# Two W1 quarters and all keys and values of a batch in single runs of TensorE, from the third batch on

## The chip, the cores and the metric

The kernel runs on one core of one Trainium2 chip. The metric is the device time of one execution in microseconds (us). A core has five engines that run side by side, each through its own queue in order: TensorE (PE; its weight loads are listed as PEld), VectorE (DVE), ScalarE (ACT), GpSimd (POOL) and SyncE (SP), which here issues the DMA transfers.

## The reference

Three layers are computed one after the other for 8 batches of 576 tokens, in float32.

```python
# attention over 32 memory slots per head (8 heads of 64)
a = exp(phi - max_s(phi));  a = a / (sum_s(a) + 1e-9)
k_m = einsum('bhsm,bhsd->bhmd', a, k)
v_m = einsum('bhsm,bhsd->bhmd', a, v)
attn = softmax(q @ k_m^T / sqrt(64))
x = (attn @ v_m) as [batch, 576, 512]
# first layer block
xn = (x - mean) / sqrt(var + 1e-6) * g_ln
x = x + relu(xn @ w_ch1) @ w_ch2          # 512 -> 2048 -> 512
# second block: h = gelu(x @ w_in); u, v = halves of h
out = x + (u * (w_sg @ norm(v) + b_sg)) @ w_out
```

## The kernel before, in words

The kernel has two phases. Phase 1 does attention and the first block; phase 2 the second block. The change touches phase 1 alone.

**The stream of matmuls.** Phase 1 folds the attention's output projection into the weights: for each batch, the batch's values v_m are multiplied with W1 (scaled by g_ln and centred), in four quarters of 512 columns, by `make_vw`. The result, the tiles `VW`, is the weight of the first layer: `m1(j, c)` computes 128 hidden columns of a block of 256 or 320 tokens (six matmuls into `ph`, line 557), `m2` the second layer (three matmuls per token tile into a bank `py`, lines 587 to 589), three steps (LAG) behind `m1`. A batch has two blocks of 16 steps. The steps of all batches follow each other in one long stream on PE. In a batch from 1 to 6 each block goes through all four quarters, in the order TURNS (0, 1, 2, 3 in even batches, 3, 2, 1, 0 in odd ones), so the last two quarters of one batch are the first two of the next, and their W1 tiles stay in SBUF. The other two are loaded anew by `load_wc` (two tiles of 512 KB for a quarter; the pool has four such tiles, two quarters).

**The preparation of a batch** is spread between these steps. Every piece of it has a time in units of a plan, 18 units to a batch: `at_time(time, function)`, and `run_until` calls what is due between two steps. For batch b: `load_phi` and `load_kv` (keys and values of the first 512 tokens, four tiles n = 0 to 3, two transfers each), `load_rem` (the last 64 of the 576 tokens, "kvr"), `prep_max` (transposes into pt), `prep_exp` (mb, then exp), `prep_sum` (sums of the exponentials on POOL, two transposes into ptsum, then reciprocals rs), `prep_kv` for each half g of the heads (k_m and v_m into kvp, divided by the sums in `prep_norm`), `prep_T` (ptk, giving kvT), the scores `t_scores`, `t_norm`, `t_attn`, `t_x` (px) of each group of query tiles, and `make_vw` for each quarter.

**Small parts of the array.** Most matmuls use the whole 128 x 128 array. Three kinds use parts: `t_scores` and `make_vw` eight parts of 64 rows and 32 columns, `prep_kv` four parts of 128 rows and 32 columns for the first 512 tokens (c = 0 to 3) and, for the last 64 tokens (c = 4), parts of 64 rows, rows 64 g to 64 g + 63 of the tiles phir and kvr. These operands are plain float32, and each matmul shows as two instructions in the trace. So a W1 quarter is 16 instructions, one half of keys and values 40 (32 and then 8). All instructions of such a run are made to wait for the same things (`add_manual_dep`), so that it stands together.

**Banks.** PSUM has eight banks: two for `ph` (ps_h), four for `py` (ps_y, tags y0 to y3; the tile t of 128 tokens uses bank t mod 4), and two, pool ps_a with the one tag "a", that all of the preparation shares in the order of the plan: pt, mb, ptsum, kvp and ptk take one of them, px one, the scores and a W1 quarter both. A tile gets its bank when the tile that had it before has been read for the last time. A W1 quarter is evicted by one ACT copy (line 514) and one DVE subtraction (line 515) for each of its two banks, and cleared ahead of its run by two small DVE memsets (line 499, "claims").

**Order.** The order of instructions on each engine is made from the order of the program by a scheduler that simulates the run; `tc.issue_after(x)` keeps an instruction behind x on its engine. So an engine's order is fixed in the program that runs, and an engine waits where a semaphore is late.

Of the kernel before, what the change touches and what calls it, by code (L numbers as in the profile page):

```python
# [28 lines left out]
def fused_kernel(ctx: ExitStack, tc: tile.TileContext, q, k, v, phi, g1, w1, w2, w_in, g2, w_sg, b_sg, w_out, out):  # L29
# [5 lines left out]
    DM = H * D  # L35
# [16 lines left out]
    LAG = 3  # L52
    BESIDE = 7
    SCALE = 1.0 / math.sqrt(D)

# [85 lines left out]
    def phase1():  # L141
# [32 lines left out]
        def load_phi(b, gs):  # L174
            if gs[0] == 0:
                st["phi", b] = (
                    at.tile([P, H, 4, NM], F32, tag="phi", name="phi"),
                    at.tile([P, 4, NM], F32, tag="phir", name="phir"),
                )
            ph, pr = st["phi", b]  # L180
            hs = slice(4 * gs[0], 4 * gs[-1] + 4)
            with behind_w2(b, 5):
                load(ph[:, hs], phi[b, hs, 0:4 * P, :].rearrange("h (p c) m -> p h c m", c=4))
                for g in gs:
                    load(pr[REM * g:REM * g + REM], phi[b, 4 * g:4 * g + 4, 4 * P:S, :].rearrange("h p m -> p h m"))

        def load_kv(b, g, part):
            n = 2 * g + part
            if b == 0 and n >= 2:
                t = tail.tile([P, 2, 4, 2, D], F32, tag="vw", name="kv", bufs=VTAIL)  # L190
            else:
                t = at2.tile([P, 2, 4, 2, D], F32, tag="kv", name="kv")
            hs = slice(4 * g, 4 * g + 4)
            ins = []
            with behind_w2(b, 7 + n):
                for i, src in enumerate((k, v)):
                    src = src[b, hs, 0:4 * P, :].rearrange("h (p c) d -> p h c d", c=4)
                    ins.append(load(t[:, i], src[:, :, 2 * part:2 * part + 2, :]).ins.name)
            st["kv", b, g, part] = t, ins
# [40 lines left out]
        def prep_max(b, gs):  # L240
# [4 lines left out]
            with tc.issue_after(st["hl"].ins) if b else ExitStack():  # L245
                V.tensor_reduce(out=pm, in_=ph[:, hs].rearrange("p h c m -> p h m c"), axis=AX.X, op=ALU.max)
                for i, g in enumerate(gs):
                    rows, sub = slice(REM * g, REM * g + REM), slice(4 * i, 4 * i + 4)
                    V.tensor_tensor(out=pm[rows, sub], in0=pm[rows, sub], in1=pr[rows], op=ALU.max)
            pt = ps_of(b, [P, n, P], "pt")  # L250
# [9 lines left out]
        def prep_exp(b, gs):  # L260
# [5 lines left out]
            for i, g in enumerate(gs):  # L266
                rows, sub = slice(REM * g, REM * g + REM), slice(4 * i, 4 * i + 4)
                V.tensor_tensor(out=pr[rows], in0=pr[rows], in1=mb[rows, sub], op=ALU.subtract)
            rows = slice(REM * gs[0], REM * gs[-1] + REM)
            A.activation(ph[:, hs], ph[:, hs], AF.Exp)  # L270
            A.activation(pr[rows], pr[rows], AF.Exp)

        def prep_sum(b):
# [5 lines left out]
            for g in range(2):  # L279
                rows, sub = slice(REM * g, REM * g + REM), slice(4 * g, 4 * g + 4)  # L280
                G.tensor_tensor(out=sm[rows, sub], in0=sm[rows, sub], in1=pr[rows], op=ALU.add)
            pt = ps_of(b, [P, 2, P], "ptsum")
# [7 lines left out]

        def prep_kv(b, g):
            ph, pr = st["phi", b]
            kvp = ps_a.tile([P, 2, D], F32, tag="a", name="kvp")
            ts = [st.pop(("kv", b, g, part)) for part in range(2)]
            lands = [n for t in (*ts, st["kvr", b]) for n in t[1]] if b else []
            rows = slice(REM * g, REM * g + REM)
            for c in range(5):
                for j in range(4):
                    mm = PE.matmul(  # L299
                        kvp[32 * j:32 * j + 32],  # L300
                        ph[:, 4 * g + j, c, :] if c < 4 else pr[rows, j, :],
                        ts[c // 2][0][:, :, j, c % 2, :] if c < 4 else st["kvr", b][0][rows, :, j, :],
                        start=(c == 0),
                        stop=(c == 4),
                        skip_group_check=True,
                    )
                    for n in lands:
                        tc.add_manual_dep(mm.ins, n, ORDER, reason="all of the group together")
            if b == 0:
                st["kvp", g] = kvp  # L310
            else:
                prep_norm(b, g, kvp)

# [32 lines left out]
        def t_q(gr, i):  # L346
# [14 lines left out]
            else:  # L361
# [3 lines left out]
                )  # L365

        def t_scores(gr):
            w, b = gr["w"], gr["b"]
# [5 lines left out]
            claims = [V.memset(t[:, 0:2], 0.0).ins.name for t in sc] if b else []  # L374
            for kT, cs in parts:
                for j in range(4):
                    for g in range(2):
                        rs_, ms = slice(64 * g, 64 * g + 64), slice(32 * j, 32 * j + 32)
                        mm = PE.matmul(sc[g][ms, cs], kT[rs_, ms], qT[rs_, j, cs], start=True, stop=True, skip_group_check=True)
                        for name in claims:  # L380
                            tc.add_manual_dep(mm.ins, name, ORDER, reason="all eight parts of the array together")
            nb = 2 * w // 32
# [111 lines left out]

        def make_vw(b, turn):
            fb = TURNS[b % 2][turn]
            ws, vT = WC[fb], st["kvT", b][0][:, 1, :]
            ps = [ps_of(b + turn, [P, DM], "pvw") for _ in range(HK)]
            claims = [V.memset(t[:, 0:2], 0.0).ins.name for t in ps] if b + turn else []
            claims += st.pop(("wc", fb), [])  # L500
            for j in range(KC):
                for g in range(HK):
                    rs_, ms = slice(64 * g, 64 * g + 64), slice(32 * j, 32 * j + 32)
                    mm = PE.matmul(ps[g][ms, :], vT[rs_, ms], ws[j // 2][rs_, j % 2, :], start=True, stop=True, skip_group_check=True)  # L504
                    for n in claims:
                        tc.add_manual_dep(mm.ins, n, ORDER, reason="all eight parts of the array together")
            VW[b, fb] = []
            for g in range(HK):
                if (NFB * b + turn) % VQ in VMAIN:
                    t = vmain.tile([P, 2, DM], F32R, tag="w", name="vw")  # L510
                else:
                    t = tail.tile([P, 2, DM], F32R, tag="vw", name="vw", bufs=VTAIL)
                h, l = t[:, 0, :], t[:, 1, :]
                A.copy(h, ps[g])  # L514
                V.tensor_tensor(out=l, in0=ps[g], in1=h.bitcast(F32), op=ALU.subtract)
                VW[b, fb].append((h, l))

# [28 lines left out]
        def m1(j, c):  # L546
# [7 lines left out]
            for g in range(HK):  # L554
                wh, wl = VW[b, fb][g]
                for w_, x in ((wh, ah), (wh, al), (wl, ah)):
                    PE.matmul(ph, w_[:, ks], x[:, g, 0:w], start=(n == 0), stop=(n == 3 * HK - 1))  # L557
                    n += 1
# [52 lines left out]
        for b in range(B):  # L611
# [11 lines left out]
            for n, gs in enumerate([[0], [1]] if b == 0 else [[0, 1]]):  # L623
                at_time(pb - 5 * f, load_phi, b, gs)
# [4 lines left out]
            at_time(pb - 2 if b == 0 else pb + 0.6 * f, load_rem, b)  # L629
            for g in range(2):  # L630
                at_time(pb + kv_at[g] * f, prep_kv, b, g)
                for part in range(2):
                    n = 2 * g + part
                    at_time(pb - 4 + n if b == 0 else pb + (0.5 * part if g == 0 else kv_at[0] + 0.1 + 0.01 * part) * f, load_kv, b, g, part)
            if b == 0:
# [4 lines left out]
            for fb in range(NFB):  # L640
                if b:
                    vw_at = 18 * b + ((-10.8, -6.8, -4.2, -1.7) if b % 2 else (-10, -5.3, -3.3, -1.3))[fb]
                    vw_at = max(vw_at, first + 0.5 + 2.2 * fb + 0.7 * (b == 1 and fb == 1))
                    if fb > 1:
                        at_time(vw_at - 2.5, load_wc, TURNS[b % 2][fb])
                    at_time(vw_at, make_vw, b, fb)
            for gi, (items, base) in enumerate(zip(groups, bases)):
# [41 lines left out]
        for fb in range(NFB):  # L689
            at_time((-26.5, -26.2, -2.5, 2.0)[fb], load_w1, fb)  # L690
            at_time((-16.5, -5.0, 3.0, 7.5)[fb], scale_w1, fb)
            at_time((-16.4, -0.3, 4.6, 9.1)[fb], center_w1, fb)
            at_time((-15, 1.3, 5.8, 10.3)[fb], make_vw, 0, fb)
            at_time((1.4, 3.0, 7.4, 12.0)[fb], store_w1, fb)
# [379 lines left out]
```

## Time and profile before

| | us |
|---|---|
| median of 3 runs (1217.89 to 1219.61) | 1218.11 |
| the profiled execution | 1217.86 |
| its span in the trace | 1216.1 |
| PE busy | 1178.5 (97%) |
| DVE, ACT, POOL busy | 692.4, 465.8, 400.6 |

The profile is one execution. Its page has the busy time of each engine, the time line in 40 slices, the chain of work that ended last and the groups of instructions by line; the trace behind it answers for single stretches, lines and tiles. Times in it are us from the start of the span. A matmul's listed duration includes the filling and emptying of the array, and consecutive matmuls overlap; what one costs in a stream is the distance from its start to the next start.

### The profile page before, as it was taken

How to read it: one execution, taken by the hardware profiler on the slowest of the kernel's cores; microseconds unless marked ns; L12 is line 12 of the kernel's file. 1: busy time of each engine (PE TensorE's matmuls, PEld its weight loads, DVE VectorE, ACT ScalarE, POOL GpSimd, SP SyncE). 2: the span in 40 equal slices, each digit the busy share in tenths (PEclk: the TensorE clock that was granted, in tenths of full speed). 3: DMA queues.
4: the chain of work that ended last, by engine and by line, in shares of the span. 5: the costliest groups of instructions: out<-in, count | busy, mean ns of one | idle time of the engine just before them, and what ended most of it. 6: DMA issues, size and time to landing. Idle time of an engine off the chain costs nothing.

```text
span 1216.1 us, 20760 instructions
## 1 busy us (share of the span) xinstructions
PE 1178.5 (97%) x7711; PEld 986.2 (81%) x7711; DVE 692.4 (57%) x1669; ACT 465.8 (38%) x1064; POOL 400.6 (33%) x621
## 2 busy tenths in 40 slices
PE   4599999999999999999999999999999999999998
PEld 2277678878787878888778788889989988998997
DVE  3787665654754545744536546568576367447632
ACT  3575333222332223332223345445444354344430
POOL 2033212211110211211211212456566475656641
PEclk9599999999999999999999999999999999999999
DMA  8996544344413353513332234132250042023202
GB/s 201 270 293 180 164 109 121 95 118 103 105 57 107 82 143 91 131 53 93 84 96 69 81 102 128 35 81 71 78 148 27 19 131 86 1 73 94 78 18 70
DMA packets 199141, 124.15 MB, mean 102 GB/s; under 512 B 93312, under 2 KB 174336, under 8 KB 199040
## 3 DMA queue, kind: packets, MB, share of 16 engines
q1 hardware_dynamic: 199040, 122.82, 36.9%
q8 instruction: 61, 1.00, 0.3%
q14 instruction: 40, 0.33, 0.1%
HBM read 99.72 MB, written 31.33 MB: 108 GB/s over the span
## 4 chain that ended last, share of the span: by engine, by line
PE 88%; DVE 5%; DMA 4%; SPq 1%; issue 1%; ACT 1%; POOL 1%; DVEq 0%; POOLq 0%; ACTq 0%
PE ph L557 16%; PE py L587 11%; PE py L589 11%; PE py L588 10%; PE pvs L976 8%; PE po L999 8%; PE pv L867 8%; PE pu L951 7%; PE pvw L504 2%; PE kvp L299 2%; DMA raw<-in_moe_w_ch_dram 1%; SPq L83 1%; DMA q<-q_d 1%; PE cm L482 1%; PE px L435 1%
## 5 line engine op out<-in xcount | busy, mean ns | idle before, releaser
L557 PE MATMUL ph<-aTh,vw 128*128 128x320 f32 (+1 forms) x1024 | 244.6, 301 | 3.6 <-ACT vw L514 1.7
L587 PE MATMUL py<-whl,hh 128*128 128x512 f32 x512 | 204.5, 401 | 2.8 <-ACT hh L543 2.8
L588 PE MATMUL py<-whl,hh 128*128 128x512 f32 x512 | 202.0, 395 | 0.0
L557 PEld LDWEIGHTS ph<-aTh,vw 128*128 128x128 f32 x1024 | 177.6, 190 | 26.9 <-issue 9.1
L589 PE MATMUL py<-whl,hl 128*128 128x512 f32 x512 | 188.7, 398 | 0.0
L543 ACT ACTIVATE hh<-ph 128x256 fp32r<-128x256 f32 x256 | 97.2, 384 | 155.1 <-PE ph L557 88.0
L544 DVE SCALAR_TENSOR_TENSOR hl<-ph,hh 128x256 fp32r<-128x256 f32 x256 | 106.6, 420 | 83.4 <-ACT hh L543 82.1
L557 PE MATMUL ph<-aTl,vw 128*128 128x256 f32 (+1 forms) x512 | 152.6, 298 | 0.0
L587 PEld LDWEIGHTS py<-whl,hh 128*128 128x128 f32 x512 | 96.3, 188 | 32.9 <-issue 9.8
L976 PE MATMUL pvs<-wsh,vhl 128*128 128x288 f32 x576 | 120.9, 295 | 0.0
L588 PEld LDWEIGHTS py<-whl,hh 128*128 128x128 f32 x512 | 96.6, 189 | 20.8 <-issue 3.4
L951 PE MATMUL pu<-yTh,whl 128*128 128x288 f32 x512 | 110.9, 295 | 0.3 <-DVE ug L856 0.3
L557 PEld LDWEIGHTS ph<-aTl,vw 128*128 128x128 f32 x512 | 97.4, 190 | 10.0 <-issue 2.1
L589 PEld LDWEIGHTS py<-whl,hl 128*128 128x128 f32 x512 | 92.0, 189 | 15.4 <-issue 4.4
L976 PEld LDWEIGHTS pvs<-wsh,vhl 128*128 128x128 f32 x576 | 94.1, 188 | 0.6
L867 PE MATMUL pv<-whl,yTh 128*128 128x512 f32 x288 | 90.8, 395 | 0.0
L999 PE MATMUL po<-whl,gh 128*128 128x512 f32 x288 | 90.1, 391 | 0.0
L951 PEld LDWEIGHTS pu<-yTh,whl 128*128 128x128 f32 x512 | 85.1, 188 | 1.8 <-DVE ug L856 0.8
L543 ACT ACTIVATE cr<-ph 128x64 fp32r<-128x64 f32 x128 | 28.5, 222 | 127.2 <-PE ph L557 126.8
L976 PE MATMUL pvs<-wsl,vhl 128*128 128x288 f32 x256 | 75.4, 295 | 0.0
L951 PE MATMUL pu<-yTl,whl 128*128 128x288 f32 x256 | 75.4, 295 | 0.0
L979 POOL TENSOR_TENSOR gt<-gt,ug 128x288 f32<-128x288 f32 x64 | 52.9, 827 | 68.4 <-DVE gt L978 65.6
(153 smaller groups left out, 2165.4 us busy)
## 6 DMA issues: line engine op xcount, KB each, us to landing
wc<-w_d SPq DMA_DIRECT2D x28, 512.0 KB, 5.0
y_d<-x SPq DMA_DIRECT2D x36, 256.0 KB, 2.8
yt<-y_d SPq DMA_DIRECT2D x36, 256.0 KB, 2.7
yr<-y_d SPq DMA_DIRECT2D x36, 256.0 KB, 3.0
kv<-in_k_dram SPq DMA_DIRECT2D x32, 256.0 KB, 4.0
kv<-in_v_dram SPq DMA_DIRECT2D x32, 256.0 KB, 4.5
raw<-in_moe_w_ch_dram SPq DMA_DIRECT2D x32, 256.0 KB, 8.7
raw<-in_moe_w_ch_dram SPq DMA_DIRECT2D x16, 512.0 KB, 6.2
```

The source lines that it names most:

```text
L299: mm = PE.matmul(kvp[32 * j:32 * j + 32], ph[:, 4 * g + j, c, :] if c < 4 else pr[rows, j, :], ts[c // 2][0][:, :, j, c % 2, :] if c < 4 e ...
L543: high = A.activation(out_h, src, AF.Relu)
L544: return high, V.scalar_tensor_tensor(out=out_l, in0=src, scalar=0.0, in1=out_h.bitcast(F32), op0=ALU.max, op1=ALU.subtract)
L557: PE.matmul(ph, w_[:, ks], x[:, g, 0:w], start=(n == 0), stop=(n == 3 * HK - 1))
L587: PE.matmul(py, hh, wh, start=start, stop=False)
L588: PE.matmul(py, hh, wl, start=False, stop=False)
L589: PE.matmul(py, hl, wh, start=False, stop=stop)
L867: PE.matmul(pv, y[:, kc, cs], w, start=(n == 0), stop=(n == 3 * KC - 1))
L951: PE.matmul(pu, w[:, ds_], y[:, kc, cs], start=(n == 0), stop=(n == 3 * KC - 1))
L976: PE.matmul(pvs, v_, w_, start=(n == 0), stop=(n == len(ops) - 1))
L979: G.tensor_tensor(out=gt, in0=gt, in1=ug, op=ALU.mult)
L999: PE.matmul(po, gg[:, dc, cs], w, start=(n == 0), stop=(n == 3 * KC - 1))
```

## The change

From the third batch on (b = 2 to 7):

- `make_vw(b, turns)` takes two quarters at a time, at the time of the second one, in one run. The second quarter writes the two shared banks as before; the first writes two of the second layer's banks, y[(t0 + g) mod 4], where t0 is the first tile of the batch. The eviction is a step of its own, `evict_vw`: the second quarter's at once, the first one's 0.6 units (APART) later.
- `prep_kv(b, [0, 1])` computes both halves in one run into one bank, preceded by the ptsum transposes (`turn_sum`), at 7.0 units after the batch's start of preparation; before, the halves stood at 4.4 and 8.4 (even) or 5.2 and 7.4 (odd). Every second load of keys and values goes to a tile of wpool, so that four tiles are at hand, and the four loads stand at 0.5 + 1.2 n.
- These runs and the scores are kept behind the latest `m1` matmul (`issue_after(R["ph"].ins)`).

In all batches the last 64 tokens have 128 rows: phir becomes `prz`, [128, 2, 4, 32], cleared once at the start by POOL; half g has its values in its own 64 rows of prz[:, g] and zeros in the others, and all 128 rows of kvr are streamed. exp runs once for each half. Batches 0 and 1 keep a run for each quarter and each half. To make room, the constant `mean` becomes one column that is read 128 times. load_phi of batch 3 moves from 5 to 4.3 units ahead.

```diff
-    mean = const.tile([P, P], F32, name="mean")
-    G.memset(mean, 1.0 / DM)
+    mcol = const.tile([P, 1], F32, name="mcol")
+    G.memset(mcol, 1.0 / DM)
+    mean = mcol.to_broadcast([P, P])
+        prz = at.tile([P, 2, 4, NM], F32, name="prz")
+        G.memset(prz, 0.0)
...
+            elif b > 1 and part == 1:
+                t = wpool.tile([P, 2, 4, 2, D], F32, tag="w", name="kv")
...
-            A.activation(pr[rows], pr[rows], AF.Exp)
+            for g in gs:
+                rows = slice(REM * g, REM * g + REM)
+                A.activation(pr[rows, g], pr[rows, g], AF.Exp)
...
+        def prep_kv(b, gs):
+            kvps = ps_a.tile([P, 2, 2, D], F32, tag="a", name="kvp")
+            with tc.issue_after(R["ph"].ins) if b > 1 else ExitStack():
+                if b > 1:
+                    turn_sum(b)
+                for g in gs:
+                    for c in range(5):
+                        for j in range(4):
+                            mm = PE.matmul(
+                                kvps[32 * j:32 * j + 32, g],
+                                ph[:, 4 * g + j, c, :] if c < 4 else prz[:, g, j, :],
+                                ts[g][c // 2][0][:, :, j, c % 2, :] if c < 4 else st["kvr", b][0][:, :, j, :],
...
+        def make_vw(b, turns):
+            vT, t0 = st["kvT", b][0][:, 1, :], b // 2 * TPP + 4 * (b % 2)
+            for turn in turns:
+                if turn < turns[-1]:
+                    ps = [ps_y.tile([P, DM], F32, tag=f"y{(t0 + g) % TB}", name="pvw") for g in range(HK)]
+                else:
+                    ps = [ps_of(b + turn, [P, DM], "pvw") for _ in range(HK)]
...
+            claims = [V.memset(t[:, 0:2], 0.0).ins.name for _, ps in runs for t in ps] if b + turns[0] else []
+            with whole(b):
+                for fb, ps in runs:
+                    for j in range(KC):
+                        for g in range(HK):
+                            mm = PE.matmul(ps[g][ms, :], vT[rs_, ms], ws[j // 2][rs_, j % 2, :], start=True, stop=True, skip_group_check=True)
+        def evict_vw(b, turn):
+            for ps, (h, l) in zip(st.pop(("vw", b, turn)), VW[b, TURNS[b % 2][turn]]):
+                A.copy(h, ps)
+                V.tensor_tensor(out=l, in0=ps, in1=h.bitcast(F32), op=ALU.subtract)
...
+                    elif fb % 2:
+                        at_time(vw_at, make_vw, b, [fb - 1, fb])
+                        at_time(vw_at, evict_vw, b, fb)
+                        at_time(vw_at + APART, evict_vw, b, fb - 1)
```

## Rows read from the trace of the kernel before

**Rows 1.** The page: busy us, share of the span and instructions of each engine.
```profile
PE 1178.5 (97%) x7711; PEld 986.2 (81%) x7711; DVE 692.4 (57%) x1669; ACT 465.8 (38%) x1064; POOL 400.6 (33%) x621
```
**Rows 2.** Busy times by stretch, batches 2 to 7: length, engines, PE clock, DMA share, GB/s.
```profile
180.00:703.00 523.00, 522.47 (x3766) 423.83 (x3765) 278.82 (x748) 164.70 (x433) 85.89 (x155) 1.00 0.36 95
```
**Rows 3.** Waits of PE, 180 to 760 us: total us, times, longest.
```profile
PE ph L557 <- DVE cr L544: 0.5, 1, 0.5
```
**Rows 4.** Timeline of PE around a W1 quarter: start us, duration us, instruction.
```profile
406.94 0.39 PE L588 MATMUL py<-whl,hh 128*128 128x512 f32 x1
...
407.85 0.39 PE L589 MATMUL py<-whl,hl 128*128 128x512 f32 x1
408.17 1.09 PE L504 MATMUL pvw<-wc,kvT 64*32 64x512 f32 x16
...
409.41 0.28 PE L557 MATMUL ph<-aTl,vw 128*128 128x256 f32 x1
409.53 0.40 PE L557 MATMUL ph<-aTh,vw 128*128 128x256 f32 x2
```
**Rows 5.** Timeline of PE around two runs of scores.
```profile
387.66 0.40 PE L587 MATMUL py<-whl,cr 128*128 128x512 f32 x1
387.99 0.66 PE L379 MATMUL sc<-qT,kvT 64*32 64x256 f32 x16
...
388.92 0.39 PE L589 MATMUL py<-whl,cr 128*128 128x512 f32 x1
...
465.42 0.39 PE L587 MATMUL py<-whl,hh 128*128 128x512 f32 x1
465.73 0.46 PE L379 MATMUL sc<-qT,kvT 64*32 64x64 f32 x32
...
466.34 0.28 PE L557 MATMUL ph<-aTl,vw 128*128 128x256 f32 x1
```
**Rows 6.** Timeline of PE around one half of keys and values.
```profile
537.43 0.39 PE L588 MATMUL py<-whl,cr 128*128 128x512 f32 x1
537.75 1.08 PE L299 MATMUL kvp<-kv,phi 128*32 128x128 f32 x32
538.76 0.42 PE L299 MATMUL kvp<-kvr,phir 64*32 64x128 f32 x8
...
539.36 0.31 PE L557 MATMUL ph<-aTl,vw 128*128 128x320 f32 x1
539.51 0.45 PE L557 MATMUL ph<-aTh,vw 128*128 128x320 f32 x2
```
**Rows 7.** W1 matmuls in 200 to 700 us: count, duration ns min/median/max, first and last start.
```profile
L504 PE MATMUL pvw<-wc,kvT x384: 589/601/613, 220.6 to 698.2; 64*32 64x512 f32 x192
```
**Rows 8.** Weight loads of the W1 runs and of the mean, same columns.
```profile
L504 PEld LDWEIGHTS pvw<-wc,kvT x512: 102/106/153, 47.0 to 697.8; 64*32 64x32 f32 x171
...
L482 PEld LDWEIGHTS cm<-wc,mean x32: 187/190/338, 36.0 to 122.3; 128*128 128x128 f32 x32
```
**Rows 9.** Timelines of POOL and of SP's queue at the start.
```profile
2.77 0.52 POOL L155 MEMSET VBl<- 128x512 f32 x1
...
3.40 0.60 SPq L83 DMA_DIRECT2D phir<-in_phi_dram  x1
```
**Rows 10.** Evictions of the W1 quarters: count, duration ns min/median/max, first and last start.
```profile
L514 ACT CAST vw<-pvw x64: 560/587/607, 51.1 to 699.4; 128x512 fp32r<-128x512 f32 x64
L515 DVE TENSOR_TENSOR vw<-pvw,vw x64: 653/681/693, 51.7 to 700.1; 128x512 fp32r<-128x512 f32 x64
```
**Rows 11.** Timeline of PE: first and last of nine users of the shared banks.
```profile
414.62 0.38 PE L252 MATMUL pt<-ident,pm 128*128 128x128 f32 x2
...
456.40 1.09 PE L504 MATMUL pvw<-wc,kvT 64*32 64x512 f32 x16
```
**Rows 12.** py matmuls of line 587 up to 444.3 us, same columns as rows 7.
```profile
L587 PE MATMUL py<-whl,hh x257: 387/393/796, 54.9 to 443.8; 128*128 128x512 f32 x129
...
L587 PE MATMUL py<-whl,cr x32: 389/393/497, 164.3 to 398.3; 128*128 128x512 f32 x32
```

More of the change, by code (lines that the diff above doesn't have):

```diff
@@ L53, in fused_kernel @@
     BESIDE = 7
+    APART = 0.6
     SCALE = 1.0 / math.sqrt(D)
@@ L177, in load_phi @@
                     at.tile([P, H, 4, NM], F32, tag="phi", name="phi"),
-                    at.tile([P, 4, NM], F32, tag="phir", name="phir"),
+                    prz,
                 )
@@ L184, in load_phi @@
                 for g in gs:
-                    load(pr[REM * g:REM * g + REM], phi[b, 4 * g:4 * g + 4, 4 * P:S, :].rearrange("h p m -> p h m"))
+                    load(pr[REM * g:REM * g + REM, g], phi[b, 4 * g:4 * g + 4, 4 * P:S, :].rearrange("h p m -> p h m"))
         def load_kv(b, g, part):
@@ L248, in prep_max @@
                     rows, sub = slice(REM * g, REM * g + REM), slice(4 * i, 4 * i + 4)
-                    V.tensor_tensor(out=pm[rows, sub], in0=pm[rows, sub], in1=pr[rows], op=ALU.max)
+                    V.tensor_tensor(out=pm[rows, sub], in0=pm[rows, sub], in1=pr[rows, g], op=ALU.max)
             pt = ps_of(b, [P, n, P], "pt")
@@ L280, in prep_sum, with turn_sum @@
                 rows, sub = slice(REM * g, REM * g + REM), slice(4 * g, 4 * g + 4)
-                G.tensor_tensor(out=sm[rows, sub], in0=sm[rows, sub], in1=pr[rows], op=ALU.add)
+                G.tensor_tensor(out=sm[rows, sub], in0=sm[rows, sub], in1=prz[rows, g], op=ALU.add)
+            st["sm", b] = sm
+            if b < 2:
+                turn_sum(b)
+        def turn_sum(b):
+            sm = st["sm", b]
             pt = ps_of(b, [P, 2, P], "ptsum")
@@ L289, in prep_sum @@
             st["rs", b] = rs
[L291 to L312, printed above, removed]
+        def prep_kv(b, gs):
+            ph, _ = st["phi", b]
+            kvps = ps_a.tile([P, 2, 2, D], F32, tag="a", name="kvp")
+            ts = {g: [st.pop(("kv", b, g, part)) for part in range(2)] for g in gs}
+            lands = [n for t in (*(t for g in gs for t in ts[g]), st["kvr", b]) for n in t[1]] if b else []
+            with tc.issue_after(R["ph"].ins) if b > 1 else ExitStack():
+                if b > 1:
+                    turn_sum(b)
+                for g in gs:
[5 more added lines that the diff above has]
+                                ts[g][c // 2][0][:, :, j, c % 2, :] if c < 4 else st["kvr", b][0][:, :, j, :],
+                                start=(c == 0),
+                                stop=(c == 4),
+                                skip_group_check=True,
+                            )
+                            for name in lands:
+                                tc.add_manual_dep(mm.ins, name, ORDER, reason="all of the group together")
+            for g in gs:
+                if b == 0:
+                    st["kvp", g] = kvps[:, g]
+                else:
+                    prep_norm(b, g, kvps[:, g])
@@ L365, in t_q, with whole @@
                 )
+        def whole(b):
+            return tc.issue_after(R["ph"].ins) if b > 1 else ExitStack()
         def t_scores(gr):
@@ L374, in t_scores @@
             claims = [V.memset(t[:, 0:2], 0.0).ins.name for t in sc] if b else []
[L375 to L381, printed above, removed]
+            with whole(b):
+                for kT, cs in parts:
+                    for j in range(4):
+                        for g in range(2):
+                            rs_, ms = slice(64 * g, 64 * g + 64), slice(32 * j, 32 * j + 32)
+                            mm = PE.matmul(sc[g][ms, cs], kT[rs_, ms], qT[rs_, j, cs], start=True, stop=True, skip_group_check=True)
+                            for name in claims:
+                                tc.add_manual_dep(mm.ins, name, ORDER, reason="all eight parts of the array together")
             nb = 2 * w // 32
@@ L493, in load_wc @@
             st["wc", fb] = [load(WC[fb][n], w_d[fb][:, 2 * n:2 * n + 2, :]).ins.name for n in range(2)]
[L495 to L501, printed above, removed]
-                for g in range(HK):
[L503 to L516, printed above, removed]
@@ new lines, in make_vw @@
+        def make_vw(b, turns):
+            vT, t0 = st["kvT", b][0][:, 1, :], b // 2 * TPP + 4 * (b % 2)
+            runs = []
+            for turn in turns:
+                fb = TURNS[b % 2][turn]
+                if turn < turns[-1]:
+                    ps = [ps_y.tile([P, DM], F32, tag=f"y{(t0 + g) % TB}", name="pvw") for g in range(HK)]
+                else:
+                    ps = [ps_of(b + turn, [P, DM], "pvw") for _ in range(HK)]
+                VW[b, fb] = []
+                for g in range(HK):
+                    if (NFB * b + turn) % VQ in VMAIN:
+                        t = vmain.tile([P, 2, DM], F32R, tag="w", name="vw")
+                    else:
+                        t = tail.tile([P, 2, DM], F32R, tag="vw", name="vw", bufs=VTAIL)
+                    VW[b, fb].append((t[:, 0, :], t[:, 1, :]))
+                st["vw", b, turn] = ps
+                runs.append((fb, ps))
+            claims = [V.memset(t[:, 0:2], 0.0).ins.name for _, ps in runs for t in ps] if b + turns[0] else []
+            for fb, _ in runs:
+                claims += st.pop(("wc", fb), [])
+            with whole(b):
+                for fb, ps in runs:
+                    ws = WC[fb]
+                    for j in range(KC):
+                        for g in range(HK):
+                            rs_, ms = slice(64 * g, 64 * g + 64), slice(32 * j, 32 * j + 32)
+                            mm = PE.matmul(ps[g][ms, :], vT[rs_, ms], ws[j // 2][rs_, j % 2, :], start=True, stop=True, skip_group_check=True)
+                            for n in claims:
+                                tc.add_manual_dep(mm.ins, n, ORDER, reason="all eight parts of the array together")
@@ L556, in m1 @@
                 for w_, x in ((wh, ah), (wh, al), (wl, ah)):
-                    PE.matmul(ph, w_[:, ks], x[:, g, 0:w], start=(n == 0), stop=(n == 3 * HK - 1))
+                    R["ph"] = PE.matmul(ph, w_[:, ks], x[:, g, 0:w], start=(n == 0), stop=(n == 3 * HK - 1))
                     n += 1
@@ L623, in phase1 @@
             for n, gs in enumerate([[0], [1]] if b == 0 else [[0, 1]]):
[L624 removed]
+                at_time(pb - (4.3 if b == 3 else 5) * f, load_phi, b, gs)
                 at_time(pb + 0.2 * n, prep_max, b, gs)
@@ L629, in phase1 @@
             at_time(pb - 2 if b == 0 else pb + 0.6 * f, load_rem, b)
+            if b > 1:
+                at_time(pb + 7.0 * f, prep_kv, b, [0, 1])
             for g in range(2):
-                at_time(pb + kv_at[g] * f, prep_kv, b, g)
+                if b <= 1:
+                    at_time(pb + kv_at[g] * f, prep_kv, b, [g])
                 for part in range(2):
                     n = 2 * g + part
-                    at_time(pb - 4 + n if b == 0 else pb + (0.5 * part if g == 0 else kv_at[0] + 0.1 + 0.01 * part) * f, load_kv, b, g, part)
+                    if b == 0:
+                        kv_from = pb - 4 + n
+                    elif b == 1:
+                        kv_from = pb + (0.5 * part if g == 0 else kv_at[0] + 0.1 + 0.01 * part) * f
+                    else:
+                        kv_from = pb + (0.5 + 1.2 * n) * f
+                    at_time(kv_from, load_kv, b, g, part)
             if b == 0:
```

10 lines of the change are left out of this document (6 added, 4 removed).

## The prediction

> **What bounds the kernel now.** I read the page first: TensorE (PE) is busy for 97% of the span [rows 1]. That is an average, so the stage of the change is read by itself, in the table of busy times by stretch: from 180 to 703 us, where batches 2 to 7 are prepared and computed, PE is busy for 522.47 of 523 us at the full clock of 2.4 GHz, while DVE, ACT and POOL are busy for 278.82, 164.70 and 85.89 us [rows 2]. The list of waits agrees: in 180 to 760 us PE waited once, for 0.5 us [rows 3]. So in this stage nothing but the length of PE's own stream counts, a microsecond taken out of it should be a microsecond off the end, and any new wait on PE costs its full length. The stream's normal step is read from its timeline: four steps of a 512-column py matmul take 406.94 to 407.85, 0.23 us each; a 256-column ph step, 409.41 to 409.53, takes 0.12 us [rows 4].
>
> **What a run of small parts costs.** Against these steps I price each run as the time from the last normal start before it to a normal start behind its after-effect, less the normal steps. A W1 quarter (16 instructions in eight parts of the array, so two rounds of 512 columns): 407.85 to 409.41 is 1.56, less 0.23 and 0.12, gives 1.21 us [rows 4]. Scores of 256 columns, two rounds: 387.66 to 388.92 is 1.26, less 0.46, gives 0.80. Scores of 64 columns, 32 instructions, so four rounds: 465.42 to 466.34 is 0.92, less 0.35, gives 0.57 [rows 5]. The first two differ by 0.41 us for 512 columns (two rounds of 256 more), so 0.0008 us for each column of a round; what remains is 0.39 us for the W1 run and 0.39 for the wide scores, and for the narrow ones 0.57 - 256 x 0.0008 = 0.36. Four rounds thus cost no more beside their columns than two do: **0.36 to 0.39 us is the price of entering and leaving the small parts, once for each run.**
>
> A run of keys and values: 537.43 to 539.36 is 1.93, less 0.23 and the 0.15 us of a 320-column ph step (539.36 to 539.51), gives 1.55 [rows 6], for ten rounds of 128 columns. The last two rounds have 64 rows instead of 128. With 0.0008 us a column the columns are 1.02 and the rest is 0.53; with 0.00083 (the W1 run less 0.36) they are 1.06 and the rest is 0.49. Beyond the one entry and exit that leaves 0.13 to 0.14 us for the change from 128 to 64 rows within the run.
>
> **The change part by part.** Two quarters in one run: 24 runs (384 instructions by 16 [rows 7]) become 12. The columns stay; one entry and exit goes for each pair, 0.36 to 0.39. I take 0.36, that of the run with four rounds: 12 x 0.36 = 4.3 us (4.7 at the other end). Below that I see one bound: the third round's weights might not load beside the second, then 0.11 us [rows 8] comes back for each pair and 12 x 0.25 = 3.0 us is left. Against it speaks the kv run: its first eight rounds, each with weights of its own in the same rows of the array, take 537.75 to 538.76, 1.01 us, entry into the next mode included, while eight rounds with 0.11 us of exposed load each would take about 1.7 us [rows 6, 8].
>
> The Trainium skill, "TensorE: Matmul & The Clock Gate", in its Part 3 on packing, says that a weight load overlaps running matmuls only where the row group differs; by that the pairs would give 3.0 us. The kv run has the same row group in every round and shows no such gap, so the trace disagrees with it here.
>
> Keys and values: two runs of 1.55 become one of 20 rounds without the change of rows: 2.05 + 0.39 = 2.44 or 2.12 + 0.36 = 2.48. Saved per batch 0.62 to 0.66, I take 0.64, in six batches: 3.8 us. Batch 1 keeps two runs but loses the change of rows: 2 x 0.13 = 0.3 us. In batch 0 PE stands idle around these runs anyway: nothing.
>
> The two ptsum transposes only move; I count nothing (their share in an entry is kept for the range). The scores change their place, not their number.
>
> What is added: one more exp on ACT per batch (busy for a third of the stage [rows 2]), and the clearing of prz on POOL at the start. The first phir load now waits for that. In the trace POOL is done with its clearing at 2.77 + 0.52 = 3.29 and SP issues that load at 3.40 [rows 9]; a clear of 256 columns, half of the one shown, ends at about 3.6, so SP's whole queue may start 0.2 to 0.3 us late. I count 0 to 0.3, taking 0.1. The mean column read again and again as weights: the load takes 0.19 us now [rows 8]; it reads as many elements, so I take nothing; if it doubled, two loads of mb in each of six batches would be exposed by up to 0.19 us, 2.3 us in all, which I keep for the range.
>
> Waits: the paired runs also need two second-layer banks, cleared by DVE and given back by two ACT copies of 0.59 and two DVE subtractions of 0.68 us each [rows 10]. Kept in mind below. The second pair of W1 loads now starts when the first pair of quarters is done, with SP's later issues behind it; the next pair lies at least four of the 18 units of a batch behind, some 19 us (a sixth of the 523 us of [rows 2] is a batch). Keys and values all have tiles of their own now, so the loads no longer wait for the first half's run.
>
> **Sum.** 4.3 + 3.8 + 0.3 - 0.1 = 8.3 us. The profiled execution took 1217.86 us, so 1209.6; the median of the runs, 1218.11, stands 0.25 us above it, so **1209.8 us**.
>
> **Rivals.** (1) *The borrowed banks come back late*, the case for slower. Each batch's last pair must be evicted before the batch's own first py writes that bank. In the trace the plan is not kept: batch 4's last W1 run is at 456.40 [rows 11], while the batch's first py, the 289th of its line (257 + 32 up to there), starts at 443.8 [rows 12]. Today that costs nothing, as the run only feeds the last quarter; after the change PE would stand still from 443.8 on. The lag comes from the two banks that pt, mb, scores, ptsum, kvp and W1 runs pass on in turn: from 414.62 to 456.40 there are eight steps, 5.2 us each [rows 11]. Of the users ahead of that last run the change takes four away (the first and third quarter's own runs, one kvp, the separate ptsum), which brings it forward by 4 x 5.2 = 20.8 us, to about 435.6. With 2.0 us of run and the evictions (2 x 0.59 + 2 x 0.68 = 2.5 us for each quarter, both in turn behind it 5.1 at most) the bank is free at about 442.7, 1.1 us before it is wanted. So the forecast stands, but thinly. If only three steps fall away, PE stalls by 4.1 us in each of six batches: +24.6 - 8.3, 1234 us; it is slower than before from 1.4 us of stall per batch on. If only one or two batches stall by 2 to 3 us, the time is 1212 to 1216. The Trainium skill, "TensorEngine Tiling (Array Packing)", Gotcha 1, also warns that row tiling raises the pressure on PSUM; no row here gives that a price.
>
> (2) *The weights load in the open*: 3.0 instead of 4.3 us, 1211.1 us.
>
> (3) *The run is not one run*: PE's order is made by a scheduler, and if it sets other matmuls between the two quarters or halves, only the change of rows is saved: 14 x 0.13 = 1.8 us, 1216.3 us. Against it: today's runs of 16 and 40 stand together, held by shared waits [rows 4, 6], and the change shares them over the pair.
>
> (4) *Keys and values land late for the joined run*: it waits for eight loads and not four. Rows 3 show no such wait in this stage, and four of the loads start earlier; I fold it into (1).
>
> **Chances.** Forecast 0.62; (1) in part 0.15; (1) in full 0.11; (2) 0.05; (3) 0.04; more than 2 us better than the sum, 0.03. Measurements of this kernel tell apart about 0.2%, that is 2.4 us: faster means under 1215.7, slower over 1220.5. Faster: the forecast, (2), the better case and most of (1) in part, 0.80; within: the rest of (1) in part, (3) and the mild end of (1) in full, 0.10; slower 0.10. The range: below, 9.0 us by the dearer prices, and one entry a batch if the ptsum transposes share that of the kv run, 6 x 0.39 = 2.3, so 1206.8; above, it takes in (2), (3) and most of (1) in part, 1217.
>
> **What would show it.** Right: 12 runs of 32 W1 instructions and 6 runs of 80 kv instructions in the stretch of batches 2 to 7, none with 64 rows; a paired run priced as above at 2.0 to 2.1 us, the kv run at 2.4 to 2.5; PE busy for all of that stage, and the stage shorter by about 8 us; batch 4's last pair before its first py. Wrong: a wait of py for the eviction of a W1 quarter (ACT or DVE vw) at a batch's start; a pair at 2.2 us; a stage that is shorter by 8 us while the end is not.

## The result, and the profile after

The changed kernel took 1207.50 us (median of 6 runs, 1205.89 to 1213.17), the kernel before beside it 1218.17 us (6 runs): ratio 0.9919, 95% interval 0.9906 to 0.9932. A second measurement gave 1210.40 us (6 runs) against 1217.15 us (11 runs), ratio 0.9940, 0.9923 to 0.9958. The change is 7 to 11 us faster; the mean of all 12 runs is 1209.3 us, that of all 61 runs of the kernel before 1217.7 us, 8.4 us apart. The forecast was 1209.8 us and 8.3 us.

The page of the changed kernel, busy time by engine; it answers [rows 1]:

```profile
PE 1167.4 (97%) x7711; PEld 991.3 (82%) x7711; DVE 689.7 (57%) x1669; ACT 467.1 (39%) x1071; POOL 400.7 (33%) x622
```

PE has the same 7711 instructions and is busy 11.1 us less. The stretch in which this happens can be cut out exactly, by two landmarks that both kernels have: the start of the last group of eight cm matmuls (they give the column means by which a quarter of W1 is centred; the expectations below call this the second group), and the last group of four py. From the timeline of PE, the kernel before and then the one after:

```profile
119.72 3.60 PE L482 MATMUL cm<-wc,mean 128*128 128x512 f32 x8
...
806.93 1.08 PE L589 MATMUL py<-whl,hl 128*128 128x512 f32 x4
```

```profile
116.19 3.59 PE L504 MATMUL cm<-wc,mcol 128*128 128x512 f32 x8
...
797.07 1.07 PE L624 MATMUL py<-whl,hl 128*128 128x512 f32 x4
```

Between them lie 687.2 us before and 680.9 us after: **6.3 us of the 10 us by which the two spans (1216.1 and 1206.0) differ arise here**, 3.5 ahead of it, where the change does next to nothing, and what follows is alike. The expectations below count to the very last py, which is 0.7 us behind the start of its group in each kernel.

The two runs that the change makes, in the timeline of PE after. First a pair of W1 quarters, then ptsum with the keys and values:

```profile
428.45 0.28 PE L592 MATMUL ph<-aTh,vw 128*128 128x256 f32 x1
428.66 1.95 PE L544 MATMUL pvw<-wc,kvT 64*32 64x512 f32 x32
430.53 0.39 PE L592 MATMUL ph<-aTh,vw 128*128 128x256 f32 x1
430.76 0.28 PE L592 MATMUL ph<-aTl,vw 128*128 128x256 f32 x1
```

```profile
341.51 0.31 PE L592 MATMUL ph<-aTh,vw 128*128 128x320 f32 x1
341.66 0.38 PE L297 MATMUL ptsum<-ident,sm 128*128 128x128 f32 x2
341.97 1.08 PE L315 MATMUL kvp<-kv,phi 128*32 128x128 f32 x32
342.87 0.40 PE L315 MATMUL kvp<-kvr,prz 128*32 128x128 f32 x8
343.08 1.06 PE L315 MATMUL kvp<-kv,phi 128*32 128x128 f32 x32
343.96 0.40 PE L315 MATMUL kvp<-kvr,prz 128*32 128x128 f32 x8
344.29 0.41 PE L592 MATMUL ph<-aTh,vw 128*128 128x320 f32 x1
344.54 0.31 PE L592 MATMUL ph<-aTl,vw 128*128 128x320 f32 x1
```

The pair: 428.45 to 430.76 is 2.31, less two ph steps of 0.12, gives 2.07 us; all 12 pairs come to 2.07. Keys and values: 341.51 to 344.54 is 3.03, less two ph steps of 0.15, gives 2.73 us with the transposes; less their 0.24 about 2.5 us. Both are one run each, as in [rows 4, 6] the single quarter at 1.21 and the half at 1.55 us.

New is a wait. In 185 to 760 us PE's list of waits after has one line (us in total, times, longest), where [rows 3] had 0.5 us once:

```profile
PE pt L258 <- DVE pm L255: 1.3, 2, 0.7
```

The busy times by stretch (columns as [rows 2]) show the two places, batches 4 and 6:

```profile
311.00:314.00 3.00, 2.27 (x12) 1.39 (x10) 2.68 (x9) 1.01 (x3) 0.83 (x1) 1.00 0.29 46
...
489.00:491.50 2.50, 1.88 (x9) 1.07 (x8) 2.17 (x7) 1.01 (x3) 0.56 (x1) 1.00 0.23 36
```

Priced like a run, pt takes 1.64 and 1.54 us there, instead of the 0.22 us that it takes in the other batches and in the kernel before: 2.7 us lost, more than the 1.3 us listed.

### The profile page after: what moved, and what is told of

Same layout as the page of the kernel before. It is cut to its first block, busy times and chain, and to the rows that moved or that the text cites. A ratio compares the mean times of both kernels' runs of the same rounds, so it can differ in the third digit from the quotient of the medians.

```text
span 1206.0 us, 20725 instructions
## 1 busy us (share of the span) xinstructions
PE 1167.4 (97%) x7711; PEld 991.3 (82%) x7711; DVE 689.7 (57%) x1669; ACT 467.1 (39%) x1071; POOL 400.7 (33%) x622
## 4 chain that ended last, share of the span: by engine, by line
PE 86%; DVE 5%; DMA 4%; SPq 2%; issue 1%; POOL 1%; ACT 1%; POOLq 0%; DVEq 0%
PE ph L592 16%; PE py L622 10%; PE py L624 10%; PE py L623 10%; PE pvs L1027 8%; PE po L1050 8%; PE pv L918 8%; PE pu L1002 7%; PE pvw L544 2%; DMA raw<-in_moe_w_ch_dram 2%; SPq L85 2%; PE kvp L315 1%; DMA q<-q_d 1%; PE cm L504 1%; PE sc L401 1%
## 5 line engine op out<-in xcount | busy, mean ns | idle before, releaser
L592 PE MATMUL ph<-aTh,vw 128*128 128x320 f32 (+1 forms) x1024 | 247.2, 300 | 3.5 <-ACT aTh L440 1.4
L624 PE MATMUL py<-whl,hl 128*128 128x512 f32 x512 | 183.2, 397 | 0.0
```

Source lines behind the costliest of these rows:

```text
L592: R["ph"] = PE.matmul(ph, w_[:, ks], x[:, g, 0:w], start=(n == 0), stop=(n == 3 * HK - 1))
L624: PE.matmul(py, hl, wh, start=False, stop=stop)
```

## The experiments

Times between the two landmarks are called the stretch. It is 687.2, 688.0 and 688.3 us in three profiles that compute as before, and 680.9, 681.3, 681.4, 681.4 and 681.7 us in five that compute as after (means 687.8 and 681.3).

**Are the terms of the sum right?** Pairs undone, keys and values joined:

```diff
...
-                    elif fb % 2:
-                        at_time(vw_at, make_vw, b, [fb - 1, fb])
...
+                    at_time(vw_at, make_vw, b, [fb])
...
```

> The kernel after with the pairs of W1 quarters undone: each quarter has a run of its own at the time that it has in before, in the shared banks; keys and values stay joined. Theory (one entry and exit for each run): 12 x (2 x 1.21 - 2.065) = 4.3 us slower, 1211.8 us, with 24 runs of 16 at 1.21 us. Rival (the pairing also sets the bank chain right, and undoing it makes the joined keys and values late): PE waits appear and the time is over 1214 us. Rival (pairing saves nothing, the gain comes from elsewhere): 1207.5 us.

Measured: 1213.08 us (8 runs), stretch 685.3 us, 3.9 us more than after. The 24 runs of a quarter take 29.12 us in all, the 12 pairs took 24.83: **4.29 us for the pairs**, as forecast. The stretch doesn't show this alone: one of the two waits of pt, described above, went with it, and another wait, of ph for DVE, came.

Keys and values apart, pairs kept. In this kernel the load of batch 3's remainder lands in prz before batch 2's second half has read it, so that batch 2 comes out wrong; the instructions and their sizes are the same, and only times are read from it:

```diff
...
-            if b > 1:
-                at_time(pb + 7.0 * f, prep_kv, b, [0, 1])
...
-                if b <= 1:
-                    at_time(pb + kv_at[g] * f, prep_kv, b, [g])
+                at_time(pb + kv_at[g] * f, prep_kv, b, [g])
...
```

> The kernel after with keys and values in two runs for each batch, at the times of before, and with ptsum at its old time; the 128 rows stay, and the pairs stay. Theory (an entry and exit of 0.36 us for each run, and 0.13 us for the change from 128 to 64 rows, which stays saved): 6 x (2 x 1.42 + 0.24 - 2.73) = 2.1 us slower, 1209.6 us, each run of 40 at 1.42 us. Rival (only the change of rows is worth anything): 1207.5 us. Rival (all of the 3.7 us that the joined runs save come from joining): 1211.2 us, runs of 40 at 1.55 us.

Measured: 1211.15 us (4 runs), stretch 684.3 us, 3.0 more than after; 2.0 of it are the runs (of 40 at 1.42 us), and the two waits of pt are 0.4 us shorter. The rest lies in batch 1, ahead of any run that this edit moves: a W1 quarter there takes nearly twice as long as in after. Timeline of PE in this kernel and in after, then this kernel's busy times around the run (columns as [rows 2]):

```profile
160.04 1.96 PE L541 MATMUL pvw<-wc,kvT 64*32 64x512 f32 x16 [0.76 <-issue]
```

```profile
158.08 1.09 PE L544 MATMUL pvw<-wc,kvT 64*32 64x512 f32 x16 [0.75 <-issue]
```

```profile
159.80:163.30 3.50, 3.25 (x21) 1.62 (x22) 1.35 (x4) 1.07 (x2) 0.22 (x1) 0.51 0.95 275
```

The granted clock was 0.51 in those 3.5 us, so the lower level, 1.2 GHz; in the 3.8 us before PE had been busy for 1.89. In each of the other 13 profiles this run takes 1.09 us. So about 1.3 us of the stretch belong to this one execution and not to the edit.

Both undone together, with load_phi of batch 3 at 3.6 units:

> The kernel after with both the pairs and the joined keys and values undone, at the times of before; what is left of the change are the 128 rows, the order of loads and the column of the mean (load_phi of batch 3 stands at 3.6 units so that prz isn't overwritten early). Theory: 14 x 0.13 = 1.8 us faster than before (the third rival of the prediction, the run that is not one run), and 4.3 + 2.1 = 6.4 us slower than after. Rival (the change of rows is free, and all comes from the joining): same as before. Rival (a separate ptsum and a longer chain of banks cost more): slower than before by the waits, which PE's list would show.

Measured: 1212.80 us (4 runs, ratio 0.9956, 0.9938 to 0.9973), stretch 686.5 us, 5.1 more than after and 1.3 less than before. A half of keys and values, timeline of PE in this kernel:

```profile
361.40 0.39 PE L621 MATMUL py<-whl,cr 128*128 128x512 f32 x1
361.71 1.08 PE L312 MATMUL kvp<-kv,phi 128*32 128x128 f32 x32
362.61 0.40 PE L312 MATMUL kvp<-kvr,prz 128*32 128x128 f32 x8
362.94 0.41 PE L589 MATMUL ph<-aTh,vw 128*128 128x320 f32 x1
363.20 0.30 PE L589 MATMUL ph<-aTl,vw 128*128 128x320 f32 x1
```

361.40 to 363.20 is 1.80, less 0.23 and 0.15, gives 1.42 us against 1.55 with 64 rows: **the change of rows costs 0.13 us**, as forecast. And pt doesn't wait here, while ph waits once more as in the kernel before: undoing the joins takes the new wait away, which is why less than the forecast 6.4 us is lost. With 2.7 us of pt back and 0.7 us of ph's wait added 4.4 would remain; the other 0.7 was not traced.

**Where do the 3.5 us ahead of the stretch come from?** Three theories: the order of SP's loads at the start (in after both phi loads stand ahead of both prz loads), the column of the mean, or no cause in the change: the start lands differently from one execution to the next.

> The kernel before with one edit: at the start both large phi loads are issued ahead of both remainder loads (phir), the order that SP has in the kernel after. Question: after stands 3.3 to 3.6 us earlier than before at every landmark from 116 us on (second group of eight cm matmuls at 115.96 instead of 119.49 us), ahead of the part that the prediction priced. Theory A (SP's order at the start makes this gain): about 1214.8 us instead of 1218.2, first ph matmul near 49.8 us instead of 51.7, the cm group near 116. Rival B (it comes from the single column of the mean or from the cleared remainder tile): no change, 1218.2 and 119.5. Rival C (where the start lands differs from one execution to the next): neither the order nor the mean decides, and the runs of one kernel spread over 3 us.

Measured: 1216.33 us (10 runs), ratio 0.9995, 0.9985 to 1.0004; the profiled execution reached the cm group at 117.07.

> The kernel after with the clearing of prz moved ahead of the clearing of the VB tiles on POOL, which gives SP the order of before at the start (phi, prz, phi, prz). Theory A: the 3.4 us of the start are lost, about 1210.9 us instead of 1207.5, first ph matmul near 51.7. Rival B: no change, 1207.5. Rival C: no steady difference from after.

> The kernel after with the clearing of prz first, once more, beside the others of this call: SP has the order of before at the start. The first four runs had a mean of 1210.9 us, after itself 1208.2 and 1210.3 in two calls. Theory A: mean over 1210.5 us. Theory C (the start lands differently from execution to execution, whatever the order): a mean between 1208 and 1210.5 us, as after.

Measured: 1211.42 us (4 runs) and 1210.12 us (6 runs), mean of all ten 1210.6, against 1209.3 for after; the six alone have a mean of 1210.4, in the range of theory C; and the two profiled executions reached the cm group at 115.75 and 115.44, earlier than after's.

> The kernel before with two edits: both large phi loads of the start ahead of both remainder loads, and the mean as one column that is read 128 times. No batch is computed otherwise than before. Theory A (SP's order makes the start faster) gives what the order alone gave, a mean near 1216.4 us; theory B (the column, whose clearing takes less of POOL and whose reads are otherwise the same, helps the start) gives 1214 to 1215 us; theory C (neither) 1217.4 us. The weight loads of the column: if they took longer than those of the full tile, mb and cm steps would be longer than in before (eight cm matmuls 3.60 us, mb 0.43 us beside its stream).

Measured: 1216.22 us (12 runs, mean 1216.5), cm group at 118.70 and still 3.60 us long; its weight loads take 190 ns in the median, as those of the full tile do [rows 8]. The column costs nothing and brings nothing beyond the order.

> The kernel after once more, unchanged, on the chip of the other runs of this call. In the profiles so far, where the second group of eight cm matmuls starts differs between executions of all kernels (115.75 to 119.72 us), and the time from there to the end hardly does (before 1096.4 and, with another load order at the start, 1097.0; after 1089.8 and, with another clearing order, 1090.3). Theory C (the start lands differently from one execution to the next, in every kernel alike): the median gain over before is that of the rest, about 6.6 us plus what batch 1 gains, 7 to 8 us, so a ratio of 0.9935 to 0.9945, and runs spread over 3 us or more. Theory A or B (the start of after is faster, 3.4 us): 10 to 11 us, ratio 0.991 to 0.992.

Measured: 1210.40 us, ratio 0.9940, as theory C expected; cm group at 117.39. Between 56 and 62 us the executions differ in the clock that PE was granted (last three columns: clock, DMA share, GB/s); before, after, and the kernel before with the column:

```profile
56.00:62.00 6.00, 5.12 (x18) 3.37 (x17) 5.62 (x14) 3.76 (x6) 0.00 (x0) 0.56 1.02 361
```

```profile
56.00:62.00 6.00, 6.00 (x29) 4.10 (x29) 5.42 (x14) 5.11 (x11) 1.31 (x1) 1.00 1.03 413
```

```profile
56.00:62.00 6.00, 6.00 (x19) 4.29 (x19) 5.10 (x12) 3.62 (x7) 1.29 (x1) 0.54 0.94 308
```

At 1.00 PE does 29 matmuls in these 6 us, at 0.54 it does 19. In the 14 profiles the cm group starts at 114.4 to 117.1 where this clock is 1.00, at 116.1 to 118.2 at 0.72 to 0.87, and at 117.9 to 119.7 at 0.54 to 0.59. From the first py to the cm group the six executions at 1.00, of both kernels' kinds, take 63.05 to 63.24 us, the eight others 64.70 to 66.67. In before the clock stood at 0.50 (1.2 GHz) until 61.3 us, PE being busy for 5.42 of the last 6.3 us; in after it was back at 1.00 (2.4 GHz) from 54.9 us, PE having been busy for 4.82 of the 5.9 us ahead. This part took 1.7 us longer in before than in after. The other 1.9 of the 3.5 us lie ahead of the first ph, which came at 51.69 us before and 49.82 after, and at 48.1 to 50.6 in the other profiles.

So **much of the 3.5 us is where this one execution landed**. The means leave about 2 us for the start (8.4 less 6.5 for the stretch), of which SP's order may make about 1 (1216.4 and 1216.5 against 1217.7; 1210.6 against 1209.3). With runs of after that spread over 7 us, the mean of 12 is sure to about 1.6 us, so even these 2 us stand only just clear of the scatter; what makes the rest isn't settled.

**The first rival: how late may the last pair be?** In batches 2 to 6 it is called 2.5 to 2.9 units later:

```diff
+                        vw_at = 18 * b + 1.2 if fb == 3 and b < 7 else vw_at
```

> The kernel after with the last pair of batches 2 to 6 called at 1.2 units after the batch's start instead of 1.3 to 1.7 before it, 12 to 14 us later. It prices the first rival of the prediction. In after the pair of batch 4 starts at 428.7, its last eviction ends near 433, and the first py of the batch comes about 6.4 us behind its first ph at 436.3, so near 442.7: some 10 us of slack, where the prediction reckoned 1.1. Rival (1) as a mechanism: PE stands still in front of the first py for 1 to 4 us in each of five batches, 5 to 20 us slower than after, and the list of waits names py behind ACT or DVE vw. Against it: if the scheduler fills the gap with steps of the first layer, under 2 us.

Measured: 1209.76 us (one run), stretch 682.3 us, 1.0 more than after. Batch 4, where the pair now starts 10.4 us later than in after, then batch 6:

```profile
439.07 1.95 PE L544 MATMUL pvw<-wc,kvT 64*32 64x512 f32 x32
...
442.36 0.28 PE L592 MATMUL ph<-aTh,vw 128*128 128x256 f32 x1
442.48 0.40 PE L622 MATMUL py<-whl,hh 128*128 128x512 f32 x1
...
616.78 1.95 PE L544 MATMUL pvw<-wc,kvT 64*32 64x512 f32 x32
...
621.52 0.47 PE L622 MATMUL py<-whl,hh 128*128 128x512 f32 x1 [1.18 <-DVE sc L395]
```

In batch 4 the py follows its ph without a gap, 1.5 us behind the pair; only in batch 6, where DVE began the evictions 2.7 us behind the start of the pair (1.8 in batch 4), does py wait, for 1.2 us (the list names a small memset that ends just behind the third of DVE's four subtractions). The second reading held: with steps of the first layer in the gap, some ten microseconds of delay cost one. In after itself the place with the least room is batch 2: DVE's last subtraction ends at 259.8 us and the batch's first py starts at 261.65.

**The new wait.** DVE after, timeline, and under it PE:

```profile
307.29 1.10 DVE L379 STREAM_TRANSPOSE qT<-q 128x512 f32<-128x512 f32 x1 [1.19 <-DMA q<-q_d]
...
309.79 2.03 DVE L252 TENSOR_REDUCE pm<-phi 128x256 f32<-128x1024 f32 x1
311.74 0.70 DVE L429 STREAM_TRANSPOSE at<-z 128x512 f32<-128x512 f32 x1
312.37 0.18 DVE L579 SCALAR_TENSOR_TENSOR cr<-ph,cr 128x64 fp32r<-128x64 f32 x1
312.48 0.58 DVE L255 TENSOR_TENSOR pm<-pm,prz 64x128 f32<-64x128 f32 x2
...
312.79 0.65 PE L258 MATMUL pt<-ident,pm 128*128 128x128 f32 x2 [0.73 <-DVE pm L255]
```

The same batch before:

```profile
307.91 1.10 DVE L362 STREAM_TRANSPOSE qT<-q 128x512 f32<-128x512 f32 x1 [1.35 <-DMA q<-q_d]
...
312.96 2.06 DVE L246 TENSOR_REDUCE pm<-phi 128x256 f32<-128x1024 f32 x1
315.05 0.60 DVE L249 TENSOR_TENSOR pm<-pm,phir 64x128 f32<-64x128 f32 x2
...
323.88 0.78 DVE L388 STREAM_TRANSPOSE z<-sc 128x256 f32<-128x256 f32 x2 [1.20 <-PE sc L379]
...
327.67 0.38 PE L252 MATMUL pt<-ident,pm 128*128 128x128 f32 x2
```

Here pm are the maxima of phi, which pt transposes. DVE stood for the same load of q before, too, and pm ended 195.9 us behind the cm group, against 196.9 after. What changed is pt's turn for a bank: before, scores held both shared banks ahead of it until DVE had read them at 324.7 us, and pt came 12 us behind pm. After, the same scores start at 301.72 instead of 323.12 us, the banks are free when the plan calls pt, and DVE isn't done. First remedy: pm of batches 4 and 6 called earlier, with pt where it was.

```diff
...
-                at_time(pb + 0.2 * n, prep_max, b, gs)
+                at_time(pb + 0.2 * n - 0.3 * (b in (4, 6)), prep_max, b, gs)
+                if b in (4, 6):
+                    at_time(pb, turn_max, b, gs)
```

> The kernel after with DVE's part of prep_max (the maxima pm) of batches 4 and 6 called 0.3 units earlier, the transposes pt and all banks where they were. In after, PE waits for pm in these two batches, 1.3 us in the list of waits; with the restart the two places take 1.64 and 1.54 us instead of 0.22. Theory (this wait is the one new stall of the change, and it is a matter of 0.7 us of lead): it goes, 2.7 us faster than after at most, 2 to 2.7 us likely. Rival (another wait behind it takes its place, or DVE is late with the eviction that now comes behind pm): same time as after.

Measured: 1207.27 us, stretch 681.7 us, pt 1.67 and 1.50 us in the two places: a miss. pm stood behind the same transpose of q on DVE as before:

```profile
306.32 1.09 DVE L385 STREAM_TRANSPOSE qT<-q 128x512 f32<-128x512 f32 x1 [1.20 <-DMA q<-q_d]
...
308.81 2.06 DVE L252 TENSOR_REDUCE pm<-phi 128x256 f32<-128x1024 f32 x1
...
311.52 0.58 DVE L255 TENSOR_TENSOR pm<-pm,prz 64x128 f32<-64x128 f32 x2
```

With 1.0 in place of 0.3:

> The kernel after with DVE's part of prep_max (pm) of batches 4 and 6 called 1.0 units earlier. With 0.3 units DVE's order stayed as it was, and so did PE's wait: pm stood behind a transpose of q (qT), for which DVE waited 1.2 us at 306.3 for the load of q. Now the reduction pm stands ahead of that transpose. Theory (PE waits because DVE's queue stands behind the load of q): the two places where pt takes 1.6 and 1.5 us fall back to 0.22 each, no wait of pt in the list, and the time from the second cm group to the last py, 681.9 to 682.4 less 0.5 us in four profiles of after's kind, falls by 2 to 2.7 us to about 679.5. Rival (the wait only moves, say to the scores, as the transposes qT now come later): no change in that stretch, and another line in the list of waits.

Measured: 1208.66 us, stretch 680.8 us; pt no longer waits by the list, but PE's places still take 1.23 us each, now "PE py L628 <- ACT hh L584: 0.7, 2, 0.3": half the rival's case. With 2.0:

> As the run with pm 1.0 units earlier, but 2.0 units. There pt was no longer listed as waiting, yet its two places still took 1.23 us each: the second part of pm (the remainder) stood behind the same transpose of q, and the cr of the first layer behind that, so ACT's hh and then py were late. Here both parts of pm stand ahead of all transposes of q on DVE. Theory (DVE's queue behind the load of q is the cause): both places of pt fall to 0.22 us, no wait over 0.3 us in the stretch from 185 to 760 us, and the time from the second cm group to the last py is 679.4 to 680.0 us, against 681.6 to 682.4 in the five profiles of after's kind. Rival (what stands behind the load of q is late whatever it is): another wait of 1 us or more, and 681 us or more.

Measured: **1206.28 us (6 runs, 1205.41 to 1207.70), ratio 0.9906, 0.9893 to 0.9919**, stretch 679.6 us, the fastest kernel here. PE, and what is left of its waits:

```profile
304.29 0.39 PE L630 MATMUL py<-whl,hl 128*128 128x512 f32 x1
304.52 0.38 PE L264 MATMUL pt<-ident,pm 128*128 128x128 f32 x2
304.65 0.48 PE L628 MATMUL py<-whl,hh 128*128 128x512 f32 x1
```

```profile
PE ph L598 <- DVE hl L585: 0.4, 2, 0.2
```

All six pt take 0.22 to 0.24 us. The stretch gave back 1.7 us, 0.3 short of the least expected. With pm ahead of the transposes that wait for q there is no wait, and with it behind them there is one, moved or not. But PE's order moved pt along, to 1.5 us behind the end of pm, so a plain lack of lead isn't told apart from DVE's queue; and why the load of q comes when it does was not tried.

## Why the prediction was right

- **The price of a run** was right to a hundredth: 2.07 for the pair (forecast 2.0 to 2.1), 2.5 for keys and values (2.4 to 2.5), 0.13 for the rows. Pairs 4.3 forecast and 4.29 measured; keys and values 3.8 and 3.7 (18.91 us in all for the kvp runs, one with its ptsum, and 1.18 for the other ptsum before; 16.41 together after); batch 1 0.3 and 2 x 0.13, one of them ahead of the stretch.
- **The second rival** (weights in the open) is out: it wanted 2.18 us or more for a pair. The Trainium skill, "TensorE: Matmul & The Clock Gate", Part 3, says that a weight load overlaps running matmuls only where the row group differs. The trace disagrees here: rounds three and four of the pair use the row groups of rounds one and two, and 2.07 us leave no room for a load in the open. The third rival (not one run) and the fourth (late loads) are out by the timeline and the list of waits.
- **The step that failed** is "any new wait on PE": it was looked for at the borrowed banks alone. The bank chain was thought to bring batch 4's last pair forward by 20.8 us; counted from the cm group it came 24.2 us earlier, at 428.7. Run and evictions, both in turn reckoned at 7.1 us, overlapped and took 4.3. So all four banks were free at 432.9, 6.7 us ahead of the batch's first py at 439.68 and not 1.1 (the 442.7 and the 10 us of slack in the expectation of the late pair were an estimate), and the first rival, given 0.26, did not occur. But the lag of that chain, counted only as a danger, had been the cover of pt: with it gone, 2.7 us were lost to pm, and the 0.7 us that the wait of [rows 3] cost, priced like a run, were gained. Terms and waits make 4.3 + 3.7 + 0.13 - 2.7 + 0.7 = 6.1 us, and the stretch measured 6.5 in the mean, not the 8 that the prediction named as its sign; the 0.4 left over were not traced.
- **The start** was put at 0.1 us lost. SP did not wait: the prz loads were issued together from 3.96 us, behind both phi loads, and the loads of keys at 5.26 instead of 5.34. The mean of the runs gained some 2 us there, not all explained. That the total came within 0.1 us of the forecast 8.3 is thus luck, two errors of about 2 us that cancel; the mechanism of the joined runs and its terms were right.

## What to carry to other kernels

On an engine that is never idle, price a mode by the distance from the last normal step to the next: the entry and exit come once for each run whatever its length, so joining two runs saves that price once. When a change frees a resource that has been late, ask what that lateness was covering, on the engines that feed the freed step, and what stands at the head of their queues. And compare two landmarks within the trace where the start of an execution scatters by more than the effect.

## What the runs showed of the hardware

Leaving and entering the parts of the array costs 0.36 to 0.39 us for each run beside its columns at 0.00083 us each, with 2, 4, 10 or 20 rounds in it (1.21 us for a W1 quarter, 2.07 for a pair, 1.42 for a half of keys and values, 2.5 for both); a change from 128 to 64 rows inside a run costs 0.13 us more (1.55 against 1.42). A weight operand read from one column 128 times loads as fast as a full tile (190 ns in the median, eight cm matmuls 3.59 to 3.60 us in both). And the same program lands its start 1.2 us apart: the unchanged kernel after reached the cm group at 116.19 and 117.39 us, with a granted clock of 1.00 and 0.75 between 56 and 62 us.
